# Attention kernel, one core: heads 0 to 3 in 64-key tiles of 192 queries, heads 4 to 7 with two-token value rows; first q and k in pieces of two heads, last stores by tile, at most four loads or stores under way

## Chip, cores, metric

One core of a Trainium2 chip. The metric is the device time of one execution in microseconds (us). Most numbers are of three to six timed executions, each kernel beside the kernel before on the same chip. An execution counts as slow when it is over 1.5% above the fastest of the same kernel; ratios use fast ones alone. Medians take in the slow ones.

## The reference, cut

Sliding-window attention with a linear bias, then a token-mixing layer on its output. All inputs and outputs are float32.

```python
B, H, S, D = 8, 8, 576, 64          # batches, heads, tokens, head width
scores = q @ k.T / 8                 # per batch and head
mask   = (i - j >= 0) & (i - j < 128)
attn   = softmax(where(mask, scores - slope[h] * |i - j|, -1e9))
x      = attn @ v                    # (B, S, 512), heads side by side
wq, wk = x @ w_q, x @ w_k            # (B, S, 64)
mixed  = (wq @ wk.T / 8) @ x
out    = relu(mixed) @ w_out         # (B, S, 512)
```

## The kernel before

Every operation is an object with an engine and a place in a fixed plan (a long string), so each engine runs its own operations in plan order. All of them are recorded through one helper line, which is why every row of the profile says L159 and one has to go by tile names: `ld` and `ldv` are the landing buffers of q/k and of v, `nat` and `vt` their 16-bit copies, `qT`/`kT` the transposed q and k, `pt` the exponentials, `bank` the PSUM.

```python
# q and k: 4 heads per load, 128 partitions, 2304-byte runs
nc.sync.dma_start(out=t, in_=srcs[x][b].rearrange(
    "(f i a) (g j) d -> f (a g) i (j d)", f=2, a=2, j=9)[f])
# transposes: pairs of 64-row products, 18 for a load
for j in range(9):
    for a in range(2):
        r = slice(64 * a, 64 * a + 64)
        nc.tensor.transpose(bank(bk[a]).bitcast(F16)[:, 64 * j : 64 * j + 64],
                            n[r, j].rearrange("p i d -> p (i d)"), ident[r, r])
# v: five pieces of up to 128 tokens per batch, all 8 heads in one transfer, 256-byte runs
nc.sync.dma_start(out=t[0:w], in_=v[b, :, P * kb : P * kb + w, :].rearrange("h s d -> s h d"))
# ... scores: 128-key tiles of 256 queries; exponentials of 1024 columns; bias product of 2048
# ... values: 18 products of 128 keys by 65 columns for two heads
# v and q/k are cast to 16 bits by POOL, in plan order
copy(eng, vt[b % 2][0:w, kb, :].rearrange("p (h e) -> p h e", h=H)[:, :, 0:D], t[0:w])
copy(eng, n, t.rearrange("p i (j d) -> p j i d", j=9))
# ... one store of 512 KB for every two output tiles
```

The softmax here doesn't subtract the row's maximum and nothing guards it: scores larger than these inputs give would overflow.

## Time and profile before

| | before |
|---|---|
| median of 3 | 151.2 us (149.89 to 153.47) |
| span of the profiled execution | 149.7 us, granted clock 1.00 |
| busy: PE, DVE, ACT, POOL | 125.7, 125.7, 118.5, 58.9 us |
| idle of PE by its start gaps, whole span | 29.7 us |
| DMA | 39.4 MB, mean 263 GB/s, nearly full until about 118 us |

In the page the engines stand with their busy time; the row DMA gives the busy share of the 16 DMA engines in tenths, in 40 slices of the span; the chain follows the last instruction back to what released it. Windows give busy times in a stretch. The lines themselves stand in the prediction. "Idle of PE" is worked out from the trace: the gap from one PE start to the next, less what the columns take at 2.4 a ns and less 95 ns at a change of tile shape, summed where it exceeds 30 ns.

### The profile page before, as it was taken

The page shows a single profiled execution, that of the slowest core. Times are in us where ns is not written, and L with a number is a line of the kernel's source. Part 1 is how long each engine was busy: PE and PEld are TensorE (multiplying, and loading weights), DVE is VectorE, ACT ScalarE, POOL GpSimd, SP SyncE. Part 2 cuts the span into 40 slices and gives each one's busy share as a digit, 9 for nine tenths or more (in the row PEclk, how much of TensorE's full clock was granted, in tenths as well). Part 3 has the DMA queues.
Part 4 walks back from the last instruction along what each step waited for, and adds up shares of the span by engine and source line. Part 5 has one row for each costly group of instructions (what it writes and reads, how often), then busy time and mean ns, then how long its engine had stood idle before and what let it go on. Part 6 is the DMA issues. An engine that isn't in the chain of part 4 may idle for free.

```text
span 149.7 us, 5314 instructions
## 1 busy us (share of the span) xinstructions
PE 125.7 (84%) x2308; PEld 82.6 (55%) x2308; DVE 125.7 (84%) x212; ACT 118.5 (79%) x170; POOL 58.9 (39%) x78
## 2 busy tenths in 40 slices
PE   6567388676889979889989999999789999999870
PEld 6465167555756456547466566576544757555320
DVE  5749987979999998789999989999799989994700
ACT  6959937995889868997799999959889989741560
POOL 4064137354915767333845381364341710000000
PEclk9999999999999999999999999999999999999999
DMA  4999999999999999999999999799699896033075
GB/s 151 383 327 266 180 365 351 264 171 358 389 263 191 296 299 195 236 306 309 348 348 372 338 405 227 167 254 279 157 371 340 235 385 222 4 140 144 0 314 176
DMA packets 50775, 39.40 MB, mean 263 GB/s; under 512 B 39488, under 2 KB 39488, under 8 KB 50752
## 3 DMA queue, kind: packets, MB, share of 16 engines
q1 hardware_dynamic: 50752, 39.07, 88.7%
q8 instruction: 18, 0.29, 0.8%
q14 instruction: 5, 0.04, 0.1%
HBM read 29.62 MB, written 9.44 MB: 261 GB/s over the span
## 4 chain that ended last, share of the span: by engine, by line
PE 40%; DMA 16%; DVE 13%; ACT 12%; SPq 9%; POOL 4%; issue 2%; POOLq 0%; DVEq 0%
PE bank L159 40%; DMA ld<-in_q_dram 10%; SPq L159 9%; ACT pt L159 8%; DMA ld<-in_k_dram 6%; DVE pt L159 5%; POOL nat L159 2%; ACT qT L159 2%; DVE xT L159 2%; POOL vt L159 2%; DVE x L159 2%; ACT kT L159 1%; DVE kT L159 1%; DVE osb L159 1%; DVE rm L159 1%
## 5 line engine op out<-in xcount | busy, mean ns | idle before, releaser
L159 ACT ACTIVATE pt<-bank 128x1024 f16<-128x1024 f32 x64 | 62.7, 1036 | 9.3 <-PE bank L159 9.0
L159 POOL CAST nat<-ld 128x1152 f16<-128x1152 f32 x30 | 34.2, 1146 | 36.7 <-PE bank L159 10.6
L159 DVE TENSOR_TENSOR pt<-pt,table 128x2048 f16<-128x2048 f16 x32 | 41.0, 1293 | 2.1 <-ACT pt L159 2.0
L159 PE MATMUL bank<-wout_sb,rm 128*128 128x512 f16 x128 | 31.8, 380 | 0.0
L159 POOL CAST vt<-ldv 128x512 f16<-128x512 f32 (+1 forms) x35 | 20.8, 613 | 25.4 <-DVE pt L159 15.5
L159 PE MATMUL bank<-qT,kT 64*128 64x256 f16 (+2 forms) x320 | 25.4, 267 | 4.6 <-ACT qT L159 2.0
L159 PE MATMUL bank<-vt,pt 128*128 128x65 f16 x576 | 23.7, 200 | 4.6 <-ACT pt L159 3.1
L159 PEld LDWEIGHTS <-pt 128*128 128x128 f16 x576 | 21.4, 102 | 9.7 <-issue 2.6
L159 DVE TENSOR_TENSOR x<-bank,inv 128x640 f16<-128x640 f32 x32 | 25.8, 817 | 0.8
L159 PEld LDWEIGHTS <-kT 64*128 64x128 f16 x320 | 14.5, 99 | 11.5 <-issue 8.6
L159 ACT COPY osb<-bank 128x512 f32<-128x512 f32 x24 | 13.9, 606 | 7.1 <-PE bank L159 7.1
L159 PE MATMUL bank<-ident,nat 64*128 64x64 f16 x576 | 14.7, 199 | 5.6 <-POOL nat L159 2.8
L159 PEld LDWEIGHTS <-nat 64*128 64x128 f16 x576 | 12.2, 100 | 10.1 <-POOL nat L159 4.7
L159 PEld LDWEIGHTS <-rm 128*128 128x128 f16 x128 | 10.8, 98 | 12.6 <-issue 2.5
L159 ACT COPY qT<-bank 128x1152 f16<-128x1152 f16 x12 | 13.5, 1121 | 2.6 <-PE bank L159 2.6
L159 ACT ACTIVATE rm<-bank 128x512 f16<-128x512 f32 x21 | 12.7, 610 | 2.2 <-PE bank L159 2.2
L159 DVE COPY kT<-bank 128x1152 f16<-128x1152 f16 x8 | 10.8, 1354 | 3.2 <-PE bank L159 3.2
L159 DVE COPY xT<-bank 128x640 f16<-128x640 f16 (+1 forms) x32 | 12.5, 448 | 0.4 <-PE bank L159 0.4
L159 PE MATMUL bank<-x,wkn 128*64 128x512 f16 x80 | 10.1, 383 | 0.0
L159 PE MATMUL bank<-wqT,gm 64*128 64x256 f16 x64 | 8.4, 288 | 1.5 <-DVE wqT L159 0.6
L159 ACT COPY kT<-bank 128x1152 f16<-128x1152 f16 x8 | 9.1, 1138 | 0.5 <-PE bank L159 0.5
L159 DVE TENSOR_SCALAR rm<-bank 128x512 f16<-128x512 f32 x11 | 7.5, 684 | 2.3 <-PE bank L159 2.2
(45 smaller groups left out, 112.1 us busy)
## 6 DMA issues: line engine op xcount, KB each, us to landing
ld<-in_k_dram SPq DMA_DIRECT2D x16, 576.0 KB, 6.9
ld<-in_q_dram SPq DMA_DIRECT2D x16, 576.0 KB, 7.0
ldv<-in_v_dram SPq DMA_DIRECT2D x32, 256.0 KB, 7.1
out_dram<-osb SPq DMA_DIRECT2D x16, 512.0 KB, 5.2
ldv<-in_v_dram SPq DMA_DIRECT2D x8, 128.0 KB, 7.3
osb<-in_moe_w_out_dram SPq DMA_DIRECT2D x2, 512.0 KB, 7.1
out_dram<-osbt SPq DMA_DIRECT2D x8, 128.0 KB, 3.8
osbt<-in_moe_w_q_dram SPq DMA_DIRECT2D x1, 128.0 KB, 5.3
```

What stands on the lines that cost most here:

```text
L159: r = call(*a, **k)
```

## The change

Heads 0 to 3 are to save exponentials and bias products: tiles of 64 keys by 192 queries leave 1536 score columns per two heads instead of 2048. The two heads of a pair then lie in the lower and the upper 64 partitions, so score products run on quarters of the PE array. For this v has to come by pairs of heads, one head per half of the partitions. Heads 4 to 7 take two neighbouring tokens of v in one run, 512 bytes instead of 256. The first q and k come in pieces of two heads, the last batch's output is stored tile by tile, and no more than four load or store operations are to be under way (a load of v, which is two transfers, counts as one).

```diff
-PLAN = """ ... """
+PLAN = """ ... """                      # the whole plan is new
-ldv: [P, H, D];  five loads of v per batch
+ldv: [P, S];     four loads of v per batch, of two heads each, and one small tail load
-                nc.sync.dma_start(out=t[0:w], in_=v[b, :, P * kb : P * kb + w, :].rearrange(
-                    "h s d -> s h d"))
+                for a in range(2):
+                    r = slice(64 * a, 64 * a + 64)
+                    if n < 2:
+                        nc.sync.dma_start(out=t[r].rearrange("p (s d) -> p s d", d=D),
+                                          in_=v[b, 2 * n + a].rearrange("(s p) d -> p s d", p=64))
+                    else:
+                        nc.sync.dma_start(
+                            out=t[r, 0:512].rearrange("p (m w) -> p m w", m=4),
+                            in_=v[b, 2 * n + a, 0:512].rearrange("(m p e) d -> p m (e d)",
+                                                                 p=64, e=2))
 ...                                     # transposes of q and k: 9 of 128 columns
-                        for a in range(2):
-                            r = slice(64 * a, 64 * a + 64)
-                            o = bank(bk[a]).bitcast(F16)
-                            nc.tensor.transpose(o[:, 64 * j : 64 * j + 64],
-                                                n[r, j].rearrange("p i d -> p (i d)"),
-                                                ident[r, r])
+                        nc.tensor.transpose(o[:, P * j : P * j + P],
+                                            n[:, j].rearrange("p i d -> p (i d)"), ident)
 ...                                     # scores: four products on quarters of the array
+                    for keys, t, n, w in parts[f, u]:
+                        for i in range(2):
+                            for a in range(2):
+                                r, o = slice(64 * i, 64 * i + 64), slice(64 * a, 64 * a + 64)
+                                nc.tensor.matmul(bank(bk[i])[o, w : w + n],
+                                                 kT[b % 2][r, 2 * f + a, keys],
+                                                 qT[b % 2][r, 2 * f + a, t : t + n],
+                                                 start=True, stop=True)
 ...                                     # values: 64 rows, in pairs; 34 or 36 for two heads
 ...                                     # last batch: a store for each tile of 128 tokens
+        if o.dma:                         # at most four transfers under way
+            if len(transfers) >= 4:
+                tc.add_manual_dep(o.insts[0], transfers[-4].insts[-1].name, ...)
+            transfers.append(o)
```

## The prediction

> **What bounds the kernel now.** I read the page's engine table first, then the table of windows (20 us each), then the chain, then the timeline at the start, in a busy stretch and at the end.
>
> ```profile
> PE 125.7 (84%) x2308; PEld 82.6 (55%) x2308; DVE 125.7 (84%) x212; ACT 118.5 (79%) x170; POOL 58.9 (39%) x78
> ...
> DMA  4999999999999999999999999799699896033075
> ...
> PE 40%; DMA 16%; DVE 13%; ACT 12%; SPq 9%; POOL 4%; issue 2%; POOLq 0%; DVEq 0%
> ```
> No engine stands out: PE, DVE and ACT are within five points, and DMA is full until about 118 us. The windows (busy us of PE, PEld, DVE, ACT, POOL, then clock, DMA share and GB/s) say when each matters:
>
> ```profile
> 0.00:20.00 20.00, 11.65 (x189) 9.42 (x190) 14.60 (x29) 16.72 (x23) 6.34 (x13) 1.00 0.97 271
> 20.00:40.00 20.00, 16.00 (x377) 13.01 (x376) 17.35 (x29) 14.28 (x17) 11.60 (x15) 1.00 1.06 309
> ...
> 80.00:100.00 20.00, 19.61 (x405) 13.01 (x404) 19.01 (x30) 18.95 (x29) 8.71 (x13) 1.00 0.97 284
> ...
> 120.00:140.00 20.00, 19.47 (x303) 11.48 (x303) 17.16 (x33) 12.78 (x22) 0.62 (x1) 1.00 0.44 164
> ```
> Up to 40 us the engines wait (for data); in the middle three engines are at 95% together; in the last 30 us PE alone is full. PE's busy time includes modelled ends, so I counted its idle time from start-to-start gaps instead (a gap beyond the columns at 2.4 a ns, which is 512 in 216, and beyond some 95 ns at a change of tile shape): 11 us in the first 20 us, 6 in 20 to 40, 5 in 40 to 60, 8 from 60 to 140. PE is truly bound from 60 us on. The start:
>
> ```profile
> 5.09 2.19 ACT L159 CAST nat<-ld 128x1152 f16<-128x1152 f32 x2
> ...
> 9.86 1.02 ACT L159 ACTIVATE pt<-bank 128x1024 f16<-128x1024 f32 x1 [0.70 <-PE bank L159]
> ...
> 13.16 1.23 DVE L159 TENSOR_TENSOR pt<-pt,table 128x2048 f16<-128x2048 f16 x1
> ...
> 19.43 2.26 PE L159 MATMUL bank<-vt,pt 128*128 128x65 f16 x36 [3.06 <-ACT pt L159]
> ```
> The first value product waits until 19.43, though exponentials exist from 9.86: it needs all five v pieces of the batch, and these come behind seven large q and k loads. The end is short: last output copy at 145.09, last store issued at about 146.2, end 149.7.
>
> **What the Trainium skill says.** (1) "TensorEngine Tiling (Array Packing)", Key Properties: a change of tiling mode drains the array. The trace agrees: a 128x65 value product starts 29 to 30 ns after another one, but 122 to 126 ns after the last 64-row one. I take 95 ns per change; it has 95 of them, 9 us. (2) "TensorE: Matmul & The Clock Gate", Part 3: matmuls on other row or column groups run together. It agrees: 64-row transposes start in pairs 3 ns apart and a pair takes 29.6 ns, while one full 512-column product takes 216 ns. (3) "DMA: Bandwidth & Descriptors", Specifications: line rate wants 512 B or more. It agrees: a 256 B packet of v takes 18 ns, a 2304 B one of q 93 ns (14 against 25 GB/s an engine). (4) "SBUF — State Buffer", Door 1: 64 partitions reach only half of the 16 ports. The last two stores, of 64 partitions each, show it partly: their 2048 B packets mostly take 128 ns, and 84 ns elsewhere.
>
> PE lines from which I take the durations (start, busy, group; the distance to the next start counts):
>
> ```profile
> 62.53 1.04 PE L159 MATMUL bank<-wout_sb,rm 128*128 128x512 f16 x4
> 63.40 0.71 PE L159 MATMUL bank<-vt,pt 128*128 128x65 f16 x18
> 63.95 1.02 PE L159 MATMUL bank<-wout_sb,rmt 128*128 128x512 f16 x4
> ...
> 71.77 0.44 PE L159 MATMUL bank<-ident,nat 64*128 64x64 f16 x18
> 72.04 0.38 PE L159 MATMUL bank<-qT,kT 64*128 64x256 f16 x4
> ```
> So 18 value products are 0.55 us, 18 transposes 0.27, four 512-column products 0.87.
>
> **The change part by part.** Counts are those of the instruction order of the two kernels.
>
> *ACT and DVE.* In heads 0 to 3, 64-key tiles of 192 queries leave 1536 score columns per two heads instead of 2048. Exponentials: 64 of 1.036 us (66.3) become 53 and 6 halves (54.9 + 6 x 0.6 = 58.5): -7.8. But the schedule moves copies from DVE to ACT: four relu pairs (4 x 0.85 = +3.4), three k copies and two half-partition ones (5 x 1.138 = +5.7), one q copy +1.1, one gm +0.6; smaller tables and first casts -2.6. ACT: +0.4, thus 119. DVE: 16 of 32 bias products shrink by a quarter (1.293 to about 0.98): -5.0; four k copies fewer (1.354 each) -5.4; four relu pairs fewer -3.6; gm and v casts -1.9; more setup +2. DVE: -14, thus 112. The sum of both falls from 244 to some 231 us, 5%.
>
> *PE.* Warm work before: output product 144 x 0.216 = 31.1; values 32 x 0.55 = 17.6; transposes of q and k 32 x 0.27 = 8.6; scores 64 units averaging 0.22 = 14; the G product of each batch 8 x 0.92 = 7.4; the rest (wk 4.8, wq 4.4, mixing 4.3, transposes of x 4.3) 17.8. Sum 96.5, with switches 105.5. After: values become 1120 products of 64 rows, in pairs of 29.6 ns: 32 x 0.53 = 17; even. Scores become 704 products on quarters of the array: per batch 1536 + 2048 columns at 2.4 per ns is 1.5 us, I say 1.85 with the starts of four each: 14.8; nearly even. Transposes become 30 groups of 9 with 128 columns (56 ns each, 0.50): 15.1, and four first ones of some 0.96 at a cold clock: 3.8; together +10.3. Mode changes 118: 11.2, +2.2. Sum 118, 12.5 more. The 36 warm-up products (3.8 us) go too, but they lay in idle time.
>
> *DMA.* v of heads 4 to 7 comes in 9216 packets of 512 B in place of 18432 of 256 B. On a straight line through 18 ns at 256 B and 93 at 2304, one takes 27.5 ns: saved (18432 x 18.4 - 9216 x 27.5)/16 = 5.3 us of engine time, of 133. But each v load is now two of 64 partitions, and by point (4) these may stay at 220 GB/s: 0 to 5 us saved. The limit of four transfers in flight should cost little, as the loads take 7 us to land now only because they queue.
>
> *Start.* First pieces are 288 KB instead of 576, and v00 of two heads comes seventh: before it are 2.3 MB at about 380 GB/s, 6 us, then itself 2.7 us at 220, and 2 to 3 us of latency: it lands at 11 to 12, first value product near 13 instead of 19.4. First exponential near 8. More mask work on POOL (+5 us) lies in front of the tables and should fit before 11.
>
> *End.* The last stores are 256 KB each behind its own copy and the tail tile comes earlier: 0.5 to 1 us saved.
>
> *The sum.* Take PE as a chain: before it is 6.3 (first transpose) + 105.5 + about 6 of cold clock (until 24 us a pair of transposes takes 50 to 57 ns, not 29.6) + 27 of idle = 145, then 4.7 to the end. After: first transpose at about 4.5, + 118 + some 4 cold, + idle X, + 4. That is 130.5 + X in the span, and 132 + X in measured time, which is 1.5 above the profiled span. X: of 27, the wait for v takes away about 5; lighter ACT and DVE and a fuller PE about 7 more between 20 and 110 us. X = 15, so 147.
>
> **Rivals.** *A: PE takes the whole of its extra work.* If the waits of the middle are not shortened, X stays near 22 and the time is 154. For it: PE is on 40% of the chain, 28 us of it without a break from 110 to 139. Against: the middle has 12 us of PE idle from 40 to 140 that more work can fill, and those waits are mostly for ACT and DVE, which get lighter. *B: the vector engines set the pace.* Then 5% less on them and the earlier start give 150 x 0.95 = 143. For: DVE and ACT are at 95% in 80 to 100. Against: PE idles only 1.4 us of those 20 by the gaps, and it is the one that gets more. *C: DMA sets the pace up to 118 us*; then only start and end change, and the time is 146 to 148. For: the full DMA row. Against: it is full because eight transfers queue; ideal packet times add up to some 105 us of those 118. *D: quarter-array scores are bound by weight loads.* If a set of four takes 0.15 us more than its columns, 176 sets cost 26 us and all is lost, about 160. No line of before shows a 64 by 64 product; I give it little.
>
> **Range and chances.** The middle of A, B and C is 147; I lean half a microsecond to the lower side, since a new plan was made for just these costs: 146.5. Eight times in ten between 142 and 152. The 2% borders are 148.2 and 154.2. Faster 0.58, same 0.34, slower 0.08.
>
> **What would show it.** Right: ACT near 119, DVE near 112, PE busy up in spite of fewer idle gaps; first value product before 14; q and k transposes at 0.5 us a group; v loads no faster per byte; PE on more than 40% of the chain. Wrong: value pairs above 33 ns, score sets of four far above their columns, a DMA row with gaps below 118 us (then the limit of four costs), or a first value product later than 16.

## The result, and the profile after

| | before, same rounds | after |
|---|---|---|
| median of 4 | 152.33 us (149.89 to 156.16) | 168.12 us (166.77 to 171.18) |
| span of the profiled execution | 149.7 us | 166.4 us |
| busy: PE, DVE, ACT, POOL | 125.7, 125.7, 118.5, 58.9 | 132.9, 124.0, 121.7, 70.0 us |
| idle of PE by its start gaps | 29.7 us | 36.7 us |

The ratio is 1.114 (95% interval 1.097 to 1.131): slower, against 146.5 us predicted. A ratio is the mean time of one kernel's fast runs over that of the other's of the same rounds, so not quite the ratio of the medians. The fast runs differ by some 17 us (167.67 against 150.55). The profiled executions of both kernels are fast ones.

First the page of the changed kernel: the engine table, the clock and the DMA row in 40 slices, and the chain by engine.

```profile
PE 132.9 (80%) x2930; PEld 88.1 (53%) x2930; DVE 124.0 (75%) x215; ACT 121.7 (73%) x176; POOL 70.0 (42%) x91
...
PEclk9999999997899999569999999999995999999999
DMA  5999999999999999899998799976989304423675
...
DMA 59%; PE 23%; SPq 9%; POOL 4%; issue 2%; ACT 0%; POOLq 0%
```

PE, DVE and ACT are all further from full than before (73 to 80% against 79 to 84%). The chain, which was 40% PE and 16% DMA, is now 59% DMA. The DMA row still is nearly full, and yet the mean rate fell from 263 to 237 GB/s. The bytes are the same and the span is longer, so this mean alone says little; the rates by window below say more. The clock row has dents, which the row of before has not. (No row shows the slow clock at the start: the clock's record begins with the first change to full, at 24.1 us in the kernel before and 15.9 in the changed one.)

Windows of the changed kernel (busy us of PE, PEld, DVE, ACT, POOL, then clock, DMA share and GB/s):

```profile
0.00:20.00 20.00, 10.07 (x158) 8.48 (x160) 16.39 (x42) 12.91 (x18) 14.20 (x25) 1.00 0.97 256
...
60.00:80.00 20.00, 16.35 (x359) 11.47 (x345) 14.08 (x24) 13.25 (x18) 10.99 (x13) 0.83 1.03 255
80.00:100.00 20.00, 18.20 (x464) 12.02 (x457) 16.23 (x28) 17.69 (x26) 9.83 (x11) 1.00 0.98 268
...
120.00:140.00 20.00, 16.68 (x325) 9.68 (x326) 14.10 (x23) 14.94 (x25) 2.72 (x4) 0.91 0.55 183
```

In 60 to 80 us DVE is busy for 14.1 us and ACT for 13.3, and the rate is 255 GB/s. The same window of the kernel before has 18.2, 17.6 and 316:

```profile
60.00:80.00 20.00, 18.09 (x326) 11.24 (x325) 18.24 (x32) 17.61 (x22) 10.26 (x12) 1.00 1.04 316
```

PE in the timeline of this stretch, in the changed kernel:

```profile
64.76 0.68 PE L159 MATMUL bank<-ident,nat 128*128 128x128 f16 x9
67.96 1.14 PE L159 MATMUL bank<-ident,nat 128*128 128x128 f16 x9 [2.53 <-POOL nat L159]
68.90 1.27 PE L159 MATMUL bank<-wk_sb,xT 128*128 128x64 f16 x20
```

PE waits 2.5 us for a cast of q or k, and the nine transposes that follow take 0.94 us to the next start, where warm ones take 0.52. The clock's record is at half from 67.1 to 73.9 us, so it fell during this wait. In the kernel with full transfers below the waits are shorter and the clock row has no dent. So I read the dents in the clock as a consequence of the waits; that they have no cause of their own was not tested.

The start, in the timeline (start, busy, engine, operation, and in brackets the idle time before it):

```profile
3.65 0.67 ACT L159 CAST nat<-ld 128x576 f16<-128x576 f32 x1 [1.56 <-DMA ld<-in_q_dram]
...
7.46 2.77 DVE L159 COPY table<-exps 128x1024 f16<-128x1024 f16 x6
...
10.16 1.34 DVE L159 COPY qT<-bank 64x1152 f16<-64x1152 f16 x1
...
12.22 1.09 ACT L159 ACTIVATE pt<-bank 128x512 f16<-128x512 f32 x2 [0.54 <-PE bank L159]
...
13.32 0.66 POOL L159 CAST vt<-ldv 128x576 f16<-128x576 f32 x1
...
17.18 0.95 DVE L159 TENSOR_TENSOR pt<-pt,table 128x1536 f16<-128x1536 f16 x1
...
19.77 0.69 PE L159 MATMUL bank<-vt,pt 64*128 64x65 f16 x34 [0.50 <-ACT pt L159]
```

The first pieces are there early (cast at 3.65 us, before 5.09), but six table copies hold DVE until 10.2 us, and the copy of qT stands behind them. The first exponential starts at 12.22 us, 2.4 us later than before, and the first value product at 19.77 (before 19.43). The early start was lost on DVE and in the longer chain to the first bias product (17.18 us, before 13.16). It was not lost on v: the last packet of its first load ends at 11.1 us by the trace, and its cast is done at 13.98.

PE durations in the timeline of the changed kernel:

```profile
118.15 1.22 PE L159 MATMUL bank<-vt,pt 64*128 64x65 f16 x68 [0.44 <-DVE pt L159]
...
124.34 0.68 PE L159 MATMUL bank<-ident,nat 128*128 128x128 f16 x9 [3.30 <-POOL nat L159]
```

The next PE start after the 68 value products is at 119.30, so 34 take some 0.53 us with the change of tile shape taken off; the start after the nine transposes is at 124.86, so these take 0.52. Both are as predicted.

The chain at its end, before and after (start, us, engine, tile):

```profile
100.48 8.88 DMA ld<-in_q_dram
109.51 1.16 POOL nat L159
110.72 27.95 PE bank L159 x454
```

```profile
116.88 5.55 DMA ldv<-in_v_dram
122.58 0.61 POOL vt L159
123.20 1.10 POOL nat L159
124.34 37.59 PE bank L159 x553
```

In both kernels the chain ends in a long stretch of PE that begins with the transposes of one of the last loads of q and k (in the kernel before some short links follow it, up to 145.09). After the change it begins 13.6 us later, but behind a load of k, before behind one of q; from the cast of the last k to that of the last k it is 6.4 us (116.71 and 123.14). It stands behind a load of v: POOL casts in plan order, so the cast of the last k (`nat`) stands behind that of a v piece (`vt`), which waited for its transfer.

### The profile page after: what moved, and what is told of

Same layout as the page of the kernel before. It is cut to its first block, busy times and chain, and to the rows that moved or that the text cites. A ratio compares the mean times of both kernels' runs of the same rounds, so it can differ in the third digit from the quotient of the medians.

```text
span 166.4 us, 6697 instructions
## 1 busy us (share of the span) xinstructions
PE 132.9 (80%) x2930; PEld 88.1 (53%) x2930; DVE 124.0 (75%) x215; ACT 121.7 (73%) x176; POOL 70.0 (42%) x91
## 4 chain that ended last, share of the span: by engine, by line
DMA 59%; PE 23%; SPq 9%; POOL 4%; issue 2%; ACT 0%; POOLq 0%
PE bank L159 23%; DMA ldv<-in_v_dram 21%; DMA ld<-in_q_dram 16%; DMA ld<-in_k_dram 13%; SPq L159 9%; DMA ldvt<-in_v_dram 6%; DMA osbt<-in_moe_w_q_dram 3%; POOL nat L159 2%; POOL vt L159 2%; ACT osb L159 0%; POOL wq_sb L159 0%; POOLq L159 0%
## 5 line engine op out<-in xcount | busy, mean ns | idle before, releaser
L159 ACT ACTIVATE pt<-bank 128x1024 f16<-128x1024 f32 (+1 forms) x59 | 54.6, 989 | 6.0 <-PE bank L159 6.0
L159 POOL CAST nat<-ld 128x1152 f16<-128x1152 f32 (+1 forms) x31 | 38.2, 1241 | 28.1 <-DVE pt L159 12.0
L159 DVE TENSOR_TENSOR pt<-pt,table 128x1536 f16<-128x1536 f16 (+1 forms) x32 | 42.1, 1319 | 0.7 <-ACT pt L159 0.7
L159 PE MATMUL bank<-ident,nat 128*128 128x128 f16 (+1 forms) x306 | 25.2, 241 | 15.8 <-POOL nat L159 9.1
L159 PEld LDWEIGHTS <-nat 128*128 128x128 f16 (+1 forms) x306 | 20.2, 111 | 21.4 <-POOL nat L159 11.9
L159 POOL CAST vt<-ldv 128x576 f16<-128x576 f32 (+1 forms) x31 | 20.9, 676 | 22.8 <-DMA ldv<-in_v_dram 16.0
L159 PE MATMUL bank<-vt,pt 64*128 64x65 f16 x1120 | 23.5, 192 | 6.2 <-POOL vt L159 1.5
L159 PE MATMUL bank<-qT,kT 64*64 64x64 f16 (+3 forms) x704 | 22.4, 245 | 6.6 <-DVE qT L159 2.2
L159 PEld LDWEIGHTS <-pt 64*128 64x128 f16 x1120 | 20.9, 95 | 9.3 <-issue 5.1
L159 PEld LDWEIGHTS <-kT 64*64 64x64 f16 x704 | 14.7, 112 | 13.4 <-issue 9.7
L159 PEld LDWEIGHTS <-rm 128*128 128x128 f16 x128 | 11.4, 101 | 13.6 <-issue 3.0
L159 DVE CAST wkn<-bank 128x320 f16<-128x320 f32 x8 | 3.9, 488 | 10.2 <-PE bank L159 10.1
```

The costliest lines, as they stand in the source:

```text
L159: r = call(*a, **k)
```

## The experiments

The question was what holds the loads back: the limit of four, the size of the packets, the half-partition transfers, or their number; and whether PE's extra work matters by itself. Sixteen runs, none of which beats the kernel before. The ratios are to the kernel before of the same rounds. By the fixed rule for verdicts (2%, fast runs alone) the changed kernel and the last two of section 5 are slower and the run of section 8 is the same; all the other ratios are recorded as "unclear", on two to six fast runs each, so they are worth no more than their intervals. Where a kernel is "wrong", its loads of v bring the same bytes, but of other tokens; the instructions after it are unchanged.

### 1. The limit of four, taken away and added

```diff
-            if len(transfers) >= 4:          # in the changed kernel
+            if len(transfers) >= FOREVER:
```

> The changed kernel without the limit of four transfers in flight; all else as it is. Theory L (the limit starves PE in the load phase, and the q and k of the last batch come 13 us late): 150 to 158 us, the waits of the DMA queue on loads gone, PE idle by gaps down from 37 to under 28. Rival P (PE's own 11 us more work decide): 164 or more. Rival V (v loads of 64 partitions decide): 162 or more, DMA still the chain.

Measured: correct, 165.53 us, ratio 1.095 (1.085 to 1.105). Theory L is refuted; the ranges of P and of V both hold. Set against 1.114 the limit costs about 1.7%, an estimate across different rounds whose intervals overlap. Without it the chain reads quite differently:

```profile
PE 65%; issue 10%; DVE 9%; ACT 8%; POOL 3%; DMA 2%; SPq 1%; POOLq 0%
```

while PE's idle is still 33.8 us and the span 163.2. With the limit, a late transfer hands its delay to the next through SP, and the chain runs through DMA; without it the same delay shows as waits between engines. A chain's shares tell one path, not how much each part would give back.

The converse: the same lines added to the kernel before.

> The kernel before with the limit of four transfers in flight added and nothing else. Theory L: 157 to 165 us. P and V: within 2% of before, 150 to 154.

Measured: ratio 1.013 (1.003 to 1.023); the profile fell in a slow run and is not used. So the limit is a small cost in the kernel before, and no large one in the changed kernel.

### 2. Transposes in 64-row pairs, in the changed kernel

```diff
-                        nc.tensor.transpose(o[:, P * j : P * j + P],
-                                            n[:, j].rearrange("p i d -> p (i d)"), ident)
+                        for a in range(2):
+                            r = slice(64 * a, 64 * a + 64)
+                            o = bank(bk[a]).bitcast(F16)
+                            nc.tensor.transpose(o[:, 64 * j : 64 * j + 64],
+                                                n[r, j].rearrange("p i d -> p (i d)"), ident[r, r])
```

> The changed kernel with the transposes of q and k (all but the first pieces) as pairs of 64 rows again, 0.27 instead of 0.50 us a group, 7 us less PE work. Theory L: little, 164 to 168, as PE waits in the load phase and gains only in the last 38 us, where one to no such group stands. P: 158 to 162. V: 166 to 168.

Measured: correct, 167.85 us, ratio 1.108 (1.098 to 1.119); PE's idle 38.5 us, 1.8 more, and the granted clock of the profiled execution 0.932 instead of 0.958. The 7 us taken out are mostly lost again to idle and to a slower clock. PE's work does not set the time of this kernel.

### 3. The packets of v: large or small, in one transfer or two halves

One transfer over 128 partitions with runs of 2304 bytes (wrong):

```diff
-                for a in range(2): ...                     # two halves, 256 or 512 bytes
+                nc.sync.dma_start(out=t, in_=v[b, 2 * n : 2 * n + 2].rearrange(
+                    "a (g j) d -> (a g) (j d)", j=9))
```

> The changed kernel with each v load as one transfer of 128 partitions in 2304-byte packets; the values land in wrong places, so the result is wrong on purpose. It shows what the packets and halves of v cost with the limit kept. V: 152 to 158. L: 160 to 165, as larger packets also make four in flight suffice better. P: 166 or more.

Measured: 154.52 us (151.56 to 156.52), against 150.87 for the kernel before beside it; too few fast runs for a ratio. Its two fast runs (151.56 and 153.80) are 1.9 us above the fast runs of the kernel before beside it, where the changed kernel was 17 us above. That left two readings, packet size or halves, which the next two runs separate. First the small runs in one full transfer (wrong):

```diff
+                if n < 2:
+                    nc.sync.dma_start(out=t.rearrange("p (s d) -> p s d", d=D),
+                        in_=v[b, 2 * n : 2 * n + 2].rearrange("a s d -> (a s) d").rearrange(
+                            "(s p) d -> p s d", p=P))
+                else: ...                                   # the same with 512-byte runs
```

> The changed kernel with each v load as one transfer of 128 partitions, its packets of 256 and 512 bytes kept; the values land in wrong places, wrong on purpose. If the halves of 64 partitions are the cost (theory H): 153 to 157 us, as with large packets. If the size of the packets is (theory S): 165 to 168. If both share: between.

Measured: 155.64 us, ratio 1.021 (1.006 to 1.036). Its page, engine table, clock and chain:

```profile
PE 127.6 (84%) x2930; PEld 86.0 (57%) x2930; DVE 120.4 (79%) x215; ACT 120.3 (79%) x176; POOL 66.8 (44%) x91
...
PEclk9999999999999999999999999999999999999999
...
PE 53%; DVE 22%; ACT 12%; POOL 5%; issue 5%; POOLq 0%
```

PE executes the same 2930 products. The clock row has no dent, PE's idle is 23.8 us instead of 36.7, and DMA has left the chain. The busy stretch from 60 to 120 us as one window, for the kernel before, the changed one and this one:

```profile
60.00:120.00 60.00, 56.12 (x1054) 35.37 (x1055) 56.08 (x91) 54.12 (x79) 28.21 (x35) 1.00 0.99 293
```

```profile
60.00:120.00 60.00, 52.22 (x1262) 35.47 (x1248) 47.84 (x78) 47.80 (x68) 31.29 (x36) 0.94 0.95 251
```

```profile
60.00:120.00 60.00, 56.63 (x1401) 38.28 (x1395) 52.33 (x87) 53.51 (x79) 29.54 (x37) 1.00 0.93 282
```

The last column tells it: 293, 251 and 282 GB/s, at nearly the same DMA share. The cast of the last k comes at 109.95 us instead of 123.14:

```profile
109.95 1.15 POOL L159 CAST nat<-ld 128x1152 f16<-128x1152 f32 x1
```

The second control is large runs in two halves (wrong):

```diff
+                    nc.sync.dma_start(out=t[r], in_=v[b, 2 * n + a].rearrange(
+                        "(g j) d -> g (j d)", j=9))
```

> The changed kernel with each v load as two transfers of 64 partitions, with packets of 2304 bytes; wrong values on purpose. H: 164 to 168 us. S: 153 to 157.

Measured: 163.39 us, ratio 1.089 (1.076 to 1.101), a little under H's range and far from that of S. Large packets do not save the halves, and small packets do not spoil the full transfer. Packet size is worth at most 2.5 points here (1.114 to 1.089, with intervals that overlap), the form of the transfer the rest. The waits of SP for earlier transfers, which the limit makes, clear up a trap here. The changed kernel, then the small full transfers (total us, times, longest):

```profile
SPq L159 <- DMA ldv<-in_v_dram: 13.0, 19, 1.5
SPq L159 <- DMA ld<-in_k_dram: 11.9, 9, 2.3
```

```profile
SPq L159 <- DMA ld<-in_q_dram: 19.3, 15, 2.0
SPq L159 <- DMA ld<-in_k_dram: 19.3, 17, 2.7
```

SP's waits for loads of q, k and v add up to 35.0 us in the changed kernel and 56.7 with small full transfers: the faster kernel waits longer. A long wait on a queue is no measure of its cost.

Large full transfers with no limit (wrong; the edits of the first and third experiments together):

> The changed kernel with v in large packets on 128 partitions and without the limit of four; wrong values on purpose. If loads no longer bound it, only the 11 us of extra PE work keep it from before: 150 to 154 us, no better than the 154.5 with the limit by more than 3. If the limit still starves it, 147 to 150.

Measured: 158.59 us (154.65 to 160.06), above the expected ranges, but three of four runs were slow; no ratio. It only fails to show a gain.

### 4. Halves alone, in the kernel before

```diff
-                nc.sync.dma_start(out=t[0:w], in_=v[b, :, P * kb : P * kb + w, :].rearrange(
-                    "h s d -> s h d"))
+                for a in range(w // 64):
+                    s = P * kb + 64 * a
+                    nc.sync.dma_start(out=t[64 * a : 64 * a + 64], in_=v[
+                        b, :, s : s + 64, :].rearrange("h s d -> s h d"))
```

> The kernel before with each 128-partition v load as two of 64 partitions, same 256-byte packets, result right. H: 157 to 165 us. S: within 2% of before.

Measured: correct, 164.52 us (160.13 to 167.91); one run counts as fast, 160.13 us, which is the profiled one, so there is no interval. Against the kernel before beside it (lowest 149.66, median 152.12) even that run is over 5% slower (6.5% above the mean of the fast runs beside it), and nothing changed but the cut of the v loads. The cast of the last k shows how the delay reaches the end. Kernel before, then the same with halves:

```profile
116.71 1.14 POOL L159 CAST nat<-ld 128x1152 f16<-128x1152 f32 x1
```

```profile
125.42 1.15 POOL L159 CAST nat<-ld 128x1152 f16<-128x1152 f32 x1 [0.84 <-DMA ld<-in_k_dram]
```

It comes 8.7 us later, and the span grows by 8.7 us, from 149.7 to 158.4. From this cast to the end both take 33.0 us.

### 5. What of a half costs: its place, or one transfer becoming two

Two transfers of half the heads each over all 128 partitions, in the kernel before:

```diff
+                for a in range(2):
+                    hs = slice(4 * a, 4 * a + 4)
+                    nc.sync.dma_start(out=t[0:w, hs], in_=v[
+                        b, hs, P * kb : P * kb + w, :].rearrange("h s d -> s h d"))
```

> The kernel before with each v load as two transfers, each of all its partitions and half of the heads: as many transfers and packets as with the halves of 64 partitions (80 against 72), result right. If the number of transfers is the cost (theory N): 157 to 165 us. If the halves of the partitions are (theory H): within 3% of before, 150 to 155.

Measured: correct, 157.76 us, ratio 1.038 (1.022 to 1.054). The median lies in N's range and not in H's, so in the kernel before the count alone makes up more than half of what the one fast run with halves loses (6.5%). Two transfers of 64 partitions each, the even ones and the odd ones:

```diff
+                for a in range(2 if kb < 4 else 1):
+                    s = slice(P * kb + a, P * kb + w, 2) if kb < 4 else slice(P * kb, P * kb + w)
+                    r = slice(a, P, 2) if kb < 4 else slice(0, w)
+                    nc.sync.dma_start(out=t[r], in_=v[b, :, s, :].rearrange("h s d -> s h d"))
```

> The kernel before with each v load of 128 partitions as two transfers of 64 partitions, the even and the odd ones instead of the lower and the upper half; result right. Same count and packets as with lower and upper halves. If it is the ports that lower and upper partitions share (theory H, by ports): 150 to 155 us. If any transfer of 64 partitions or the count costs: 157 to 165.

Measured: correct, 155.38 us, ratio 1.025 (1.012 to 1.038), between the two expected ranges. Twice as many transfers cost something; 64 partitions spread over the memory show no cost beyond that. The same two cuts in the changed kernel (both wrong), even and odd partitions first:

```diff
-                    r = slice(64 * a, 64 * a + 64)
+                    r = slice(a, P, 2)
```

> The changed kernel with each v load still as two transfers of 64 partitions and the same packets, but on the even and the odd partitions instead of the lower and upper half (wrong values on purpose). Ports decide: 153 to 158 us, near the 155.6 of one full transfer. Count decides: 164 to 168. Both: about 160.

Measured: 160.98 us, ratio 1.049 (1.040 to 1.058), as expected if both count; its profile fell in a slow run. Then two transfers over all partitions, half of the columns each:

```diff
+                    rows = v[b, 2 * n : 2 * n + 2].rearrange("a s d -> (a s) d")
+                    ...  out=t.rearrange("p (s d) -> p s d", d=D)[:, s]      # n < 2: 5 and 4 of 9
+                    ...  out=t[:, 256 * a : 256 * a + 256]                   # n >= 2
```

> The changed kernel with each v load as two transfers of 128 partitions with half of the columns each (wrong values on purpose). Ports decide: 153 to 158 us. Count decides: 164 to 168.

Measured: 158.96 us, ratio 1.043 (1.036 to 1.049), just above the first range. Together, with the time that the packets took, added up and divided by the 16 DMA engines, and the last cast of k from the timeline:

| kernel | v arrives as | ratio | v packets, us | q and k packets, us | last k cast at | from it to the end |
|---|---|---|---|---|---|---|
| before | one full transfer | 1 | 46.8 | 58.2 | 116.71 | 33.0 |
| before | two full | 1.038 | 45.0 | 58.6 | 121.13 | 35.2 |
| before | even and odd | 1.025 | 45.6 | 58.0 | 120.05 | 33.2 |
| before | lower and upper | 1.065, one fast run | 50.7 | 59.3 | 125.42 | 33.0 |
| changed | one full transfer | 1.021 | 39.9 | 57.9 | 109.95 | 41.5 |
| changed | two full | 1.043 | 39.9 | 58.8 | 114.31 | 42.7 |
| changed | even and odd | 1.049 | (slow profile) | | | |
| changed | lower and upper | 1.114 | 48.3 | 62.5 | 123.14 | 43.3 |
| changed, no limit | lower and upper | 1.095 | 53.0 | 61.2 | 120.78 | 42.4 |

(v packets are all of 256 and 512 bytes, which takes in 1.1 us of the two small weights. The rows of the two kernels come from several rounds; each ratio is to the kernel before of its own.) Three things are to be seen. The packets of v take longer only in lower and upper halves, in both kernels: 8.4 us more than in one full transfer in the changed one, and those of q and k beside them 4.6 us more. The last k cast comes later with them, and also with two full transfers, by 4.4 us in both kernels, though their packets take no longer. And the time from there to the end varies little within each plan, 33.0 to 35.2 us in the kernel before and 41.5 to 43.3 in the changed one, so a delay of the last k goes into the end unshortened.

In half-microsecond slices of the trace in which only v moves, halves in the kernel before reach 228 GB/s at most, even and odd or two full transfers up to 280 (in one slice each; the next best are 242 and 253). In the changed kernel halves reach 239 and one full transfer 288. This agrees with the Trainium skill, "SBUF — State Buffer", section "Can I just issue two DMAs to hit both halves?": two transfers, one on each half, serialize, and only one that spans all 128 partitions reaches all ports. The even and odd run differs from that sentence in one point: each of its transfers has 64 partitions, and its packets are not slowed.

### 6. The two halves from two queues

```diff
+                    q_ = (nc.sync, nc.scalar)[a]
-                        nc.sync.dma_start(out=t[r]...
+                        q_.dma_start(out=t[r]...
```

> The changed kernel with the upper half of each v load issued by ACT instead of SP, so that both halves run at once; result right. H by ports: the loads of v go faster, but ACT pays 32 issues of some 0.5 us and waits in order with them: 158 to 166 us. If the time does not fall, either the halves don't mix or ACT's waits eat it; the packet times of v then tell (23 and 36 ns in the changed kernel on average, 19 and 30 with 128 partitions).

Measured: correct, 175.97 us (171.97 to 178.72), above the expected range, no ratio, profile in a slow run. The packets of v, which were to tell, take 23.3 and 38.1 ns there, no less than with one queue: no sign that the halves mix. But ACT issues in its own plan order and waits there for the limit and for buffers, so a second change comes in with the second queue, and the run decides nothing. Whether two queues could mix the halves in a plan made for it stays open.

### 7. PE's extra work

Full small transfers and transposes in 64-row pairs together (wrong):

> The changed kernel with v on 128 partitions in its small packets (wrong values on purpose) and the transposes of q and k as pairs of 64 rows. With the loads out of the way PE's own work should count: 7 us less of it. If PE decides then: 148 to 151 us against the 155.6 (fast runs 153 to 154) with the 128-column transposes. If not: 152 to 156.

Measured: 158.67 us (155.51 to 160.26), above both expected ranges, three of four runs slow; no ratio. No gain is seen, and no loss can be claimed. The cleaner test is the reverse in the kernel before:

```diff
-                        for a in range(2): ...              # 64-row pairs
+                        nc.tensor.transpose(o[:, P * j : P * j + P],
+                                            n[:, j].rearrange("p i d -> p (i d)"), ident)
```

> The kernel before with the transposes of q and k on the full array with 128 columns, 0.50 instead of 0.27 us a group; result right. If PE's work sets the pace of the kernel before: 7 us more work of which some 3 to 6 us show, 153 to 157. If the idle time of PE takes it in, or fewer changes of tile shape pay it back: 149 to 152.

Measured: correct, 154.3 us, ratio 1.015 (1.010 to 1.021), PE's idle 25.2 us instead of 29.7. By the durations 32 groups of 0.50 us instead of 0.27 are 7 us more PE work, and the trace has 114 changes of tile shape instead of 95, not fewer as the expectation thought possible: some 2 us more at 95 ns. Of these 9 us 2.3 reach the time. Idle time takes in half of them; what took in the rest was not separated.

### 8. Last stores by tile, in the kernel before

```diff
+                    if b == NB - 1:
+                        for i in range(2):
+                            nc.sync.dma_start(out=out[b, P * (t - 1 + i) : P * (t + i), :],
+                                              in_=osb[n % 3][:, i, :])
+                        return
```

> The kernel before with the last batch's two 512 KB stores as four of 256 KB, each after its own tile; result right. The prediction said 0.5 to 1 us less: 150 to 151. The last tail stores end the kernel before, so it may also be nothing.

Measured: correct, 152.26 us, ratio 0.998 (0.992 to 1.004). No difference is seen, but a gain of 1 us is within the interval.

## Why the prediction was wrong

**The step that failed first** is in the part on DMA: "But each v load is now two of 64 partitions, and by point (4) these may stay at 220 GB/s: 0 to 5 us saved." The halves were seen, with their rate, and then counted as a gain not made instead of as a loss. The mean rate of v before, by its packet times, is 207 GB/s, below 220, so such a cap could look free (the prediction does not say what it was compared with). But v before is not capped there (285 GB/s in the best half-microsecond slice of v alone), and with halves the packets of q and k take longer too. The sign that the prediction took from the trace was misread: the last two stores, of 64 partitions, do have slow packets (mean 127 ns), but the six earlier stores of the same shape mostly take 84 ns a packet, and these are part of its "elsewhere". Measured, in the changed kernel, the ratio falls from 1.114 to 1.049 when the two halves are interleaved over the partitions, 6.5 points or some 10 us of 150.5. Going on to one full transfer takes it to 1.021, a further 2.8 points or 4 us, which I put down to two transfers instead of one (the intervals, 1.040 to 1.058 and 1.006 to 1.036, nearly touch). The gain from larger packets itself was sized about right: a 512-byte packet mostly takes 27 ns (27.5 predicted), and with full transfers v takes 39.9 us of engine time instead of 46.8, so 6.9 saved against 5.3 predicted. Lower and upper halves take 48.3, so the whole gain is lost again.

**The limit of four** "should cost little": about 1.7% in the changed kernel (intervals overlap) and 1.3% in the kernel before. Nearly right.

**The PE work** was sized right: transposes 0.52 us a group, 34 value products 0.53, 118 changes of tile shape. What failed is the idle term, "X = 15, so 147": it measured 36.7 with halves and 23.8 even with full transfers. With 36.7 the prediction's own sum gives 130.5 + 36.7 = 167.2 us of span, against 166.4 measured, so the miss is all in X. The wait for v at the start did go, but a wait for exponentials took its place, and ACT and DVE did not shorten the later waits. The step also missed where the PE work lies. After the last k cast the kernel before needs 33.0 us, the changed one 43.3. With full transfers the last k is cast 6.8 us earlier than in the kernel before, and the longer rest takes 8.5 us back: 151.4 us of span against 149.7. In that rest PE has 80 output products of 512 columns from `rm` where the kernel before has 48, and at 0.216 us the 32 more are 6.9 us: the plan leaves more output work for the end.

**The start**: predicted were the first exponential near 8 us and the first value product near 13; measured 12.22 and 19.77. The landing of v was right (11.1 us, predicted 11 to 12), though by a slip: 288 KB at 220 GB/s are 1.3 us, not 2.7. The mask work was expected to "fit before 11"; the table copies on DVE until 10.2 us then stood before the copy of qT. **The end**: 0.5 to 1 us saved was predicted, and the stores alone gave none that can be seen (0.998, with 0.992 to 1.004).

**ACT** at 121.7 us against 119 was close. **DVE** at 124.0 against 112 was not, and it is 120.4 in the kernel with full transfers, so most of the miss is not from the halves. Its bias product of 1536 columns takes 0.95 us at its shortest, about as worked out, but averages 1.218 over the run (1.421 for the one of 2048 columns, before 1.293). The trace shows where: the 12 with no POOL instruction beside them average 0.95 and 1.21 us (1536 and 2048 columns), the 20 with one 1.38 and 1.55; before, only 9 of 32 had one. So the bias products got 0.8 us dearer in sum instead of 5.0 cheaper. Setup at the start (tables, memsets, a cast of `nat`) is 6.7 us more, predicted 2. No run tested the part of POOL.

**The rivals.** C, the loads set the pace up to some 118 us, held in its mechanism and had the wrong sign, because it took the loads as no slower than before. A gave 154 us by PE alone with X near 22, and with full transfers X is 23.8 and the fast runs 153.16 and 154.05; but in experiment 7 such work reaches the time by only a quarter, so the number fits better than the mechanism is shown. B, the vector engines as the pace, did not come: both got emptier as a share of the span. D was false in size: four quarter-array products of 256 columns start 3 to 4 ns apart, and at full clock the next set mostly starts 108 to 109 or 134 to 138 ns after the first, where 256 columns at 2.4 a ns take 107. So a set costs up to some 30 ns more than its columns, not 150.

Open stays what the 2.1% consist of that the changed kernel loses with full transfers: wider transposes (1.5% in the kernel before) and the limit (1.3% there) would be enough, but were not undone one by one on that version with a clear result. Open is also a correct kernel with full transfers. Every full-transfer version of the changed kernel here brings wrong tokens.

## What to carry to other kernels

When a layout gives each head its own half of the partitions, look at how the loads then land before counting what the engines save: two transfers of 64 neighbouring partitions made up some 9 of the 11% lost, and without them fewer exponentials and larger packets still gave no gain (1.021). Follow the last k of the last batch: here the time from its cast to the end varied by some 2 us within a plan, so nearly every microsecond by which the loads are late is a microsecond of the result. And judge a queue by the bytes it moves and by when its last load lands, not by its busy share or its waits.

## What the Trainium skill lacked or had wrong

- "SBUF — State Buffer": it tells that halves serialize, but not what that does to a kernel with other loads beside them. Here it is 6.5 points of the time against even and odd partitions (1.114 and 1.049). Against one full transfer v packets take 48.3 us of engine time instead of 39.9, and the full-partition packets of q and k 62.5 instead of 57.9.
- The same page, "The only way to hit all 16 ports is one transfer spanning all 128 partitions": two transfers over even and odd partitions, 64 each, had v packets of 45.6 us against 46.8 for one full transfer and 50.7 for lower and upper halves, and reached 280 GB/s in their best half microsecond. So 64 partitions that are spread over the memory are not slowed.
- "DMA: Bandwidth & Descriptors": no figure for the same bytes in twice as many transfers in a loaded queue. Here two full transfers for one cost 3.8% in the kernel before and 2.2 points in the changed one, while the packets took no longer.
- "TensorE: Matmul & The Clock Gate" puts the fall to half clock down to idle windows of some 3.4 us and, in one kernel, to frequent short idle times without giving their length. Here the clock fell during one PE wait of 2.5 us in mid-kernel; the nine transposes after it took 0.94 us instead of 0.52, and the stretch from 60 to 80 us had a clock of 0.83.
